# TensorE's order written out from chunk 4 on: whole tiles, one attention step between them, and the sums issued a chunk ahead

## The chip, the cores and the metric

The kernel runs on one core of one Trainium2 chip. Its engines are TensorE (PE, whose weight loads the profile lists as PEld), VectorE (DVE), ScalarE (ACT), GpSimd (POOL) and SyncE (SP, which issues most DMAs). Each of them takes its own instructions strictly in order; they wait for each other on semaphores. The metric is the device time of one execution in microseconds, the median over several runs.

## The reference

An attention of two parts feeds a gated feed-forward layer. q, k and v are 8 batches x 8 heads x 576 positions x 64.

```python
# coarse part: positions averaged in fours, full softmax attention over 144 of them, repeated back to 576
q_d = q.reshape(B, H, Sd, factor, D).mean(axis=3)          # k_d, v_d alike
out_up = np.repeat(sm_attn(q_d, k_d, v_d), factor, axis=2)
# local part: only |i - j| < 4, so seven neighbours of each position
scores = np.where(mask, scale * np.matmul(q, k.transpose(0, 1, 3, 2)), -1000000000.0)
out_local = np.matmul(softmax(scores), v)
x = (out_up + out_local).transpose(0, 2, 1, 3).reshape(B * S, H * D)     # 4608 tokens x 512
xn = x / np.sqrt(np.mean(x * x, axis=-1, keepdims=True) + 1e-06) * rms_g
g, val = xn @ w_gate, xn @ w_val                                          # 512 -> 1536
out = (g * (1 / (1 + np.exp(-g))) * val) @ w_out                          # 1536 -> 512
```

## The kernel before

The 4608 tokens are worked in 18 chunks of 256. A chunk's feed-forward layer (`Forward`) is cut into 12 tiles f of 128 hidden columns. Numbers are kept to more than one pass's accuracy by splitting a value into a high and a low part, so a tile has 24 first products on PE (`first`, L975: gate and value halves, four pieces of the inner dimension, three combinations of high and low each) and six second products (`second`, L1010: two halves of the tokens, three combinations). Between them stand ACT's tanh (L982), two DVE operations on the PSUM result (gate L985, product L990), ACT's high part (L996) and DVE's low part (L999). First products write one of three PSUM buffers ps_h; second products of all 12 tiles add up in two buffers ps_o, which ACT copies out (L1017) for a store (L1020). The parts hs have three buffers (LAG is 2).

While chunk c runs there, the local attention of chunk c+1 is made (`Attention`): eight scores on DVE (L757 and the sum L761), a softmax over the whole chunk (L771 to L795), eight values, each of which ACT (L804, eight small copies with a scale), DVE and POOL (L811) make in parts and DVE sums (L830); then the coarse part is added (L845), squares (L855) and a mean on PE (L862) give the norm (L866 to L896), and PE transposes x in eight pieces (`turn`, L906); ACT copies the result as the high part xh (L910), DVE takes the low part xl (L914). Only then can the chunk's first product start. The tiles x_t, up_t, q_t and prod have two buffers each, kv has four.

The coarse attention (`Coarse`) has 32 steps, one for each batch and pair of heads. One makes scores on PE (L499), a maximum (L508, L513 on DVE), exponentials (L518, ACT), turns on PE (L527), copies of them (L534, ACT), values on PE (L541), the scaling (L554, DVE) and a store to DRAM. Its q, k and v sums come by a first load on SP (L354, L358) and three accumulating DMAs each on POOL's queue (L362, `Sums`); two steps share one. Scores, turns, values, the mean and the transposes of x share three PSUM buffers ps_a. Chunks 4 to 11 carry two coarse steps each, chunk 3 one, chunks 12 to 17 none.

What sets the order: for the first three chunks a planner (`Plan`), whose choices stand as they are up to a given time. From the loop over chunks at the end of the function on (it starts at chunk index 3, the fourth), the program is only written in a likely order, with places in tiles (0.37, 3.0, 6.5, 10.4 and so on) for the attention's pieces, and the scheduler of the framework then decides the order on every engine, instruction by instruction. It may put six second products in two groups, or other work between the 24 first products of a tile.

Of the kernel before, what the change touches and what calls it, by code (L numbers as in the profile page):

```python
# [29 lines left out]
NF = DF // P  # L30
# [7 lines left out]
NCH = NU // 2  # L38
WPC = 512
LAG = 2  # L40
W_BUFS = 4
FIRST = 3
EARLY = 7
COARSE = {3: 1}
# [126 lines left out]
def attn_moe_kernel(  # L171
# [153 lines left out]
    up_dram, sums, stored = {}, {}, {}  # L325
# [109 lines left out]
    class Coarse:  # L435
# [3 lines left out]
            self.b, self.hp, self.pool, self.tag = b, hp, pool or ps_a, tag  # L439

        def steps(self):
            def low():
                if (self.b, self.hp // 2) not in sums:
                    sums[self.b, self.hp // 2] = Sums(self.b, self.hp // 2)
                self.sums = sums[self.b, self.hp // 2]
                self.scores()
                self.peak(0)
                self.peak(1)
                self.scale()
                self.powers(0)  # L450
                self.powers(1)

            def high():
                self.invert()
                for par in range(2):
                    self.turn(par)
                    self.copy(par)
                self.values()
                self.scaled()
                self.store()  # L460

            return low, high

        def plan(self, at, after=()):
            b, hp, tag = self.b, self.hp, self.tag
# [57 lines left out]
        def turn(self, par):  # L523
            tp = self.t[par] = self.pool.tile([HALF, 2, SD], FP32, name=self.tag)
            for kc in range(2):
                for c in range(2):
                    nc.tensor.transpose(  # L527
                        out=tp[:, kc, c * HALF:(c + 1) * HALF],
                        in_=self.a[par][:, c, kc * HALF:(kc + 1) * HALF],
                        identity=ident_sb[:HALF, :HALF],  # L530
                    )
# [39 lines left out]
    def window(t, s0, o0=0, o1=NO):  # L571
        b_ = t[:, :, :]
        return bass.AP(
            tensor=b_.tensor, offset=b_.offset + (s0 + o0) * D,
            ap=[b_.ap[0], [D, 2], [D, o1 - o0], [1, D]],
        )

    def bcast(ap, axis, n):
        shape = list(ap.shape)
        return ap.unsqueeze(axis).broadcast_to(shape[:axis] + [n] + shape[axis:])  # L580
# [4 lines left out]
    class Attention:  # L585
# [6 lines left out]
        def steps(self):  # L592
            def score(i):
                j, par, s0 = trio[i]
                if s0 == 0:
                    self.load_score(j, par)
                self.score(i)
                self.score_sum(i)

            def softmax():  # L600
                self.peak()
                self.less()
                self.powers()
                self.total()
                self.invert()
                self.shares()

            def value(i):
                j, par, s0 = trio[i]
                if s0 == 0:  # L610
                    self.load_value(j, par)
                self.value_scalar(i, 0)
                self.value_scalar(i, 1)
                self.value(i, "DVE", self.na, NO - self.np)
                self.value(i, "POOL", NO - self.np, NO)
                self.value_sum(i)

            def add(j):
                self.load_up(j)
                self.add_up(j)  # L620
                self.squares(j)

            def root():
                self.mean()
                self.rms()
                self.root("DVE")
                self.norm(0)
                self.norm(1)

            def turn(j):  # L630
                self.turn(j)
                self.high(j)
                self.low(j)

            todo = [(0.37 * i, lambda i=i: score(i)) for i in range(8)] + [(3.0, softmax)]
            todo += [(3.1 + 0.42 * i, lambda i=i: value(i)) for i in range(8)]
            todo += [(at, lambda j=j: add(j)) for j, at in enumerate((4.8, 6.4))]
            return todo + [(6.5, root), (10.4, lambda: turn(0)), (10.5, lambda: turn(1))]

        def plan(self, newton="POOL", before=()):  # L640
            c, np_, on_tensor, T = self.c, self.np, self.pt, due[self.c]
# [109 lines left out]
        def score(self, i):  # L751
            j, par, s0 = trio[i]
            if i == 0:
                self.sc = band.tile([P, 2, 2, US, NO], FP32, name="sc")
            q, k = self.qk[j, par]
            pr = self.pr[i] = band.tile([P, 2, NO, D], FP32, name="prod")
            nc.vector.tensor_tensor(out=pr, in0=bcast(q[:, s0:s0 + 2], 2, NO), in1=window(k, s0), op=ALU.mult)  # L757
# [50 lines left out]
        def value(self, i, engine, a, b):  # L808
            j, par, s0 = trio[i]
            p = self.sc[:, j, par, s0:s0 + 2]  # L810
            (nc.vector if engine == "DVE" else nc.gpsimd).tensor_tensor(  # L811
                out=self.pr[i][:, a:b], in0=bcast(p[:, :, a:b].rearrange("p s o -> p o s"), 3, D),
                in1=window(self.v[j, par], s0, a, b).rearrange("p s o d -> p o s d"), op=ALU.mult,
            )
# [211 lines left out]
    for fg in range(3):  # L1026
        for i in range(12):
            if i % 3 == 2 if fg < 2 else i >= 8:
                f = 4 * fg + (i // 3 if fg < 2 else i - 8)
                place[1, f] = len(pieces)  # L1030
                pieces.append(seconds[f])
            else:
                n = i - (i + 1) // 3 if fg < 2 else i
# [45 lines left out]
    coarse = [(b, hp) for b in range(B) for hp in range(KT)]  # L1079
# [4 lines left out]
    atts = [Attention(0, 1, 2, (ps_o, "ps_o")).plan("DVE")]  # L1084
    atts.append(Attention(1, 2, 2, (ps_a, "ps_a")).plan("DVE", [h.valued for h in opening] + atts[0].turns))
    done = 2 * KT
# [33 lines left out]

    att, late = atts[FIRST], []
    for c in range(FIRST, NCH):
        todo = []
        if c + 1 < NCH:
            nxt = Attention(c + 1)
            todo = nxt.steps()
            n = min(COARSE.get(c, 2), len(coarse) - done)
            for i, it in enumerate(coarse[done:done + n]):  # L1130
                at = 0.2 + 5.0 * i / n
                todo += zip((at + 0.1, at + 1.3), Coarse(*it).steps())
            done += n
            todo.sort(key=lambda t: t[0])
        fwd = Forward(att)
        for f in range(NF):
            fwd.emit(f)
            late.append((fwd, f))
            if len(late) > LAG:
                fw, g = late.pop(0)  # L1140
                fw.emit_second(g)
            while todo and todo[0][0] < f + 1:
                todo.pop(0)[1]()
        assert not todo
        att = nxt
    assert done == len(coarse)
    for fw, g in late:
        fw.emit_second(g)


# [52 lines left out]
```

## Time and profile before

| | |
|---|---|
| median of 3 runs | 1147.09 us (1144.93 to 1152.68) |
| profiled execution, first to last instruction | 1144.2 us; no other time of that execution is given |
| PE busy | 1082.0 us, 95% of the span, 8002 matmuls |
| DVE, ACT, POOL busy | 927.7, 624.1, 255.7 us |
| mean granted TensorE clock | 0.977 of full speed |
| matmuls of L975 / L1010 | 5184 / 1296 |
| DMA | 119.59 MB, 105 GB/s in the mean |

A matmul's busy time in the profile includes its pipeline, so rows of matmuls overlap: how fast they follow each other is read from their starts. The transposes of x begin 106 us into the span for the first chunk and 1082.6 us for the last. In the part of the timeline that is quoted below, the name of an operand tells the step: wg and wv belong to the first products, wo and hs to the second, qk to coarse scores, a_g with ident_sb to coarse turns, vs to coarse values, x_t with ident_sb to the transposes of x. A bracket at the end of a row gives the engine's idle time before it and what ended that.

### The profile page before, as it was taken

Reading aid. Unit: us, or ns where it says so; the run is one execution under the profiler, and the core shown is the slowest. Engines: PE = TensorE matmul, PEld = TensorE weight load, DVE = VectorE, ACT = ScalarE, POOL = GpSimd, SP = SyncE. Lnnn points to the kernel's source line nnn. Section 1 sums busy time; section 2 is a strip of 40 time slices with the busy share of each in tenths; the row PEclk is TensorE's granted clock in tenths of the full one; section 3 lists DMA queues with packets and bytes.
Section 4 is the critical chain, followed back from the end, with each engine's and each line's share of the span. In section 5 each row is a group of like instructions: output and inputs, shape, how many; then the busy total and the mean of one; then the engine's idle time right before and its main releaser. Section 6 shows DMA issues by size and latency. Waiting matters only on the chain.

```text
span 1144.2 us, 22238 instructions
## 1 busy us (share of the span) xinstructions
PE 1082.0 (95%) x8002; PEld 990.2 (87%) x8002; DVE 927.7 (81%) x1869; ACT 624.1 (55%) x2284; POOL 255.7 (22%) x317
## 2 busy tenths in 40 slices
PE   6883799999999899999999999999999999999998
PEld 4772698888899899999999999999999999999997
DVE  6787898778889989797979797979798989887432
ACT  1574673747392847474747474747475573837221
POOL 1554562334221211111111111101011020201000
PEclk9885999999999999999999999999999999999999
DMA  9985482446535353535263535222231313220000
GB/s 264 301 275 170 102 227 76 95 101 149 127 87 117 99 115 88 115 87 115 83 120 87 115 88 114 78 64 75 66 91 46 105 52 99 68 58 20 1 19 19
DMA packets 76815, 119.59 MB, mean 105 GB/s; under 512 B 26784, under 2 KB 36256, under 8 KB 76704
## 3 DMA queue, kind: packets, MB, share of 16 engines
q1 hardware_dynamic: 47520, 97.34, 28.8%
q0 software_dynamic: 8640, 15.93, 9.0%
q10 hardware_dynamic: 20544, 4.89, 2.0%
q8 instruction: 63, 1.03, 0.4%
q14 instruction: 48, 0.39, 0.1%
HBM read 106.33 MB, written 11.80 MB: 103 GB/s over the span
## 4 chain that ended last, share of the span: by engine, by line
PE 76%; DVE 9%; DMA 8%; ACT 3%; issue 3%; SPq 1%; POOL 1%; ACTq 0%; DVEq 0%; POOLq 0%
PE ps_h L975 46%; PE ps_o L1010 23%; PE ps_a L541 2%; DMA wg<-in_v_sum_dram 2%; DMA qk<-in_qk_sum_dram 2%; PE ps_a L499 2%; ACT prod L804 1%; DMA vs<-in_v_sum_dram 1%; PE ps_a L906 1%; DVE prod L757 1%; DVE o_sb L271 1%; PE ps_a L527 1%; DMA kv<-in_k_pad_dram 1%; DVE sc L761 1%; DMA up<-o_g 1%
## 5 line engine op out<-in xcount | busy, mean ns | idle before, releaser
L1010 PE MATMUL ps_o<-wo,hs 128*128 128x512 f32 x1296 | 356.0, 399 | 4.2 <-POOL hs L999 3.7
L975 PE MATMUL ps_h<-xh,wg 128*128 128x256 f32 x1728 | 348.2, 283 | 4.8 <-ACT xh L910 2.3
L975 PE MATMUL ps_h<-xh,wv 128*128 128x256 f32 x1728 | 343.0, 281 | 4.6 <-DVE sil L985 4.5
L975 PEld LDWEIGHTS ps_h<-xh,wg 128*128 128x128 f32 x1728 | 282.9, 190 | 14.2 <-ACT xh L910 3.0
L975 PEld LDWEIGHTS ps_h<-xh,wv 128*128 128x128 f32 x1728 | 281.9, 189 | 10.8 <-DVE sil L985 6.9
L804 ACT ACTIVATE prod<-kv,sc 128x64 f32<-128x64 f32 x1072 | 281.7, 408 | 13.0 <-DVE sc L795 4.8
L1010 PEld LDWEIGHTS ps_o<-wo,hs 128*128 128x128 f32 x1296 | 221.9, 188 | 41.4 <-POOL hs L999 6.2
L975 PE MATMUL ps_h<-xl,wg 128*128 128x256 f32 x864 | 244.8, 283 | 0.1
L975 PE MATMUL ps_h<-xl,wv 128*128 128x256 f32 x864 | 241.5, 280 | 0.0
L982 ACT ACTIVATE sil<-ps_h 128x256 f32<-128x256 f32 x216 | 82.9, 384 | 233.9 <-PE ps_h L975 208.8
L811 POOL TENSOR_TENSOR prod<-sc,kv 128x256 f32<-128x256 f32 x144 | 116.4, 843 | 397.4 <-DVE sc L795 175.4
L985 DVE SCALAR_TENSOR_TENSOR sil<-sil,ps_h 128x256 f32<-128x256 f32 x216 | 89.7, 415 | 103.1 <-ACT sil L982 91.0
L975 PEld LDWEIGHTS ps_h<-xl,wg 128*128 128x128 f32 x864 | 164.1, 190 | 6.9 <-issue 1.3
L975 PEld LDWEIGHTS ps_h<-xl,wv 128*128 128x128 f32 x864 | 163.6, 189 | 1.8
L996 ACT ACTIVATE hs<-sil 128x256 fp32r<-128x256 f32 x216 | 89.5, 416 | 136.9 <-DVE sil L990 122.4
L757 DVE TENSOR_TENSOR prod<-q_t,kv 128x896 f32<-128x896 f32 x140 | 151.7, 1086 | 5.6 <-DMA q_t<-in_q_band_dram 5.2
L830 DVE TENSOR_REDUCE x_t<-prod 128x128 f32<-128x896 f32 x128 | 136.8, 1077 | 23.6 <-ACT prod L804 16.4
L761 DVE TENSOR_REDUCE sc<-prod 128x14 f32<-128x896 f32 x144 | 154.5, 1077 | 0.4
L999 DVE TENSOR_TENSOR hs<-sil,hs 128x256 fp32r<-128x256 f32 x196 | 91.4, 466 | 29.5 <-ACT hs L996 29.2
L990 DVE SCALAR_TENSOR_TENSOR sil<-sil,ps_h 128x256 f32<-128x256 f32 x216 | 89.9, 416 | 8.1 <-PE ps_h L975 6.4
L362 POOL DMA_DIRECT2D qk<-in_qk_sum_dram x36 | 32.2, 895 | 187.3 <-DMA qk<-in_qk_sum_dram 111.8
L811 DVE TENSOR_TENSOR prod<-sc,kv 128x128 f32<-128x128 f32 (+2 forms) x144 | 69.5, 515 | 1.6 <-PE ps_o L826 0.8
(118 smaller groups left out, 984.3 us busy)
## 6 DMA issues: line engine op xcount, KB each, us to landing
kv<-in_k_pad_dram SPq DMA_DIRECT2D x72, 320.0 KB
kv<-in_v_pad_dram SPq DMA_DIRECT2D x72, 320.0 KB
qk<-in_qk_sum_dram POOLq DMA_DIRECT2D x36, 288.0 KB, 5.3
out_dram<-o_sb SPq DMA_DIRECT2D x36, 256.0 KB
q_t<-in_q_band_dram SPq DMA_DIRECT2D x70, 128.0 KB
vs<-in_v_sum_dram POOLq DMA_DIRECT2D x36, 144.0 KB, 3.5
qk<-in_qk_sum_dram SPq DMA_DIRECT2D x12, 288.0 KB
wo<-in_qk_sum_dram SPq DMA_DIRECT2D x2, 1152.0 KB
```

The lines of the kernel that those rows point to most:

```text
L757: nc.vector.tensor_tensor(out=pr, in0=bcast(q[:, s0:s0 + 2], 2, NO), in1=window(k, s0), op=ALU.mult)
L761: nc.vector.tensor_reduce(out=self.sc[:, j, par, s0:s0 + 2], in_=self.pr[i], axis=AX.X, op=ALU.add,)
L804: nc.scalar.activation(out=self.pr[i][:, o, s], in_=self.v[j, par][:, s0 + s + o], func=AF.Copy, scale=p[:, s, o:o + 1],)
L811: (nc.vector if engine == "DVE" else nc.gpsimd).tensor_tensor(out=self.pr[i][:, a:b], in0=bcast(p[:, :, a:b].rearrange("p s o -> p o s"), ...
L830: nc.vector.tensor_reduce(out=self.x[j][:, s0:s0 + 2, par], in_=pr.rearrange("p o s d -> p s d o"), axis=AX.X, op=ALU.add,)
L975: nc.tensor.matmul(out=self.p[f][:, t], lhsT=wi(f)[:, 0, k], rhs=xi[:, k], start=(n == 0), stop=(n == 3 * KT - 1),)
L982: nc.scalar.activation(out=self.sil[f], in_=self.p[f][:, 0], func=AF.Tanh, scale=0.5)
L985: nc.vector.scalar_tensor_tensor(out=self.sil[f], in0=self.sil[f], scalar=1.0, in1=self.p[f][:, 0], op0=ALU.add, op1=ALU.mult,)
L990: nc.vector.scalar_tensor_tensor(out=self.sil[f], in0=self.sil[f], scalar=0.5, in1=self.p[f][:, 1], op0=ALU.mult, op1=ALU.mult,)
L996: nc.scalar.activation(out=self.hs[f][:, 0], in_=self.sil[f], func=AF.Copy)
L999: (nc.gpsimd if engine == "POOL" else nc.vector).tensor_tensor(out=self.hs[f][:, 1], in0=self.sil[f], in1=self.hs[f][:, 0], op=ALU.subtract,)
L1010: nc.tensor.matmul(out=self.o[j], lhsT=lhs[:, cols], rhs=rhs(f)[:, 0], start=(f == 0 and i == 0), stop=(f == NF - 1 and i == 2),)
```

## The change

The loop over chunks now runs under a manual schedule for PE alone: PE's instructions stay in the order in which the program emits them, and the scheduler places only those of the other engines. The loop is therefore written out for PE. Each tile emits its 24 first products, then the attention step due in that slot, then six second products. Tile f's second products follow the first products of tile f+2; those of tile 10 follow tile 11's, and those of tile 11 stand behind the first tile of the next chunk. A coarse step has three slots now, scores, turns and values, two tiles apart: the first step in tiles 0, 2 and 4, the second in 4, 6 and 8. The mean and the norm come in tile 8. The eight transposes of x come as one step in tile 11, behind its first products and ahead of 12 second products; before, they stood behind tile 10. The sums of the next two coarse steps are issued one chunk ahead (`sums_for`). No computation is added or taken away.

```diff
@@ Coarse.steps
-            def low():
-                if (self.b, self.hp // 2) not in sums:
-                    sums[self.b, self.hp // 2] = Sums(self.b, self.hp // 2)
+            def score():
                 self.sums = sums[self.b, self.hp // 2]
                 self.scores()
...
-            def high():
-                self.invert()
+            def turn():
                 for par in range(2):
                     self.turn(par)
                     self.copy(par)
+                self.invert()
+
+            def value():
                 self.values()
                 self.scaled()
                 self.store()
 
-            return low, high
+            return score, turn, value
@@ Attention.steps
-            def turn(j):
-                self.turn(j)
-                self.high(j)
-                self.low(j)
+            def turn():
+                self.turn(0)
+                self.turn(1)
+                for j in range(2):
+                    self.high(j)
+                    self.low(j)
...
-            return todo + [(6.5, root), (10.4, lambda: turn(0)), (10.5, lambda: turn(1))]
+            return todo, root, turn
@@ the loop over chunks
-    att, late = atts[FIRST], []
-    for c in range(FIRST, NCH):
...
-            n = min(COARSE.get(c, 2), len(coarse) - done)
-            for i, it in enumerate(coarse[done:done + n]):
-                at = 0.2 + 5.0 * i / n
-                todo += zip((at + 0.1, at + 1.3), Coarse(*it).steps())
...
-            late.append((fwd, f))
-            if len(late) > LAG:
-                fw, g = late.pop(0)
-                fw.emit_second(g)
...
+    def sums_for(n):
+        for b, hp in coarse[n:n + 2]:
+            if (b, hp // 2) not in sums:
+                sums[b, hp // 2] = Sums(b, hp // 2)
+
+    att, before = atts[FIRST], None
+    with tc.manual_schedule(engines={mybir.EngineType.PE}):
+        for c in range(FIRST, NCH):
+            fwd = Forward(att)
+            todo, slots = [], {f: [] for f in range(NF)}
+            if c + 1 < NCH:
+                nxt = Attention(c + 1)
+                todo, root, turn = nxt.steps()
+                n = min(COARSE.get(c, 2), len(coarse) - done)
+                for at, it in zip((0, 4), coarse[done:done + n]):
+                    for f, step in zip((at, at + 2, at + 4), Coarse(*it).steps()):
+                        slots[f].append(step)
+                done += n
+                sums_for(done)
+                slots[8].append(root)
+                slots[NF - 1].append(turn)
+                todo.sort(key=lambda t: t[0])
+            for f in range(NF):
+                fwd.emit(f)
+                for step in slots[f]:
+                    step()
+                if f == 0 and before:
+                    before.emit_second(NF - 1)
+                if f >= LAG:
+                    fwd.emit_second(f - LAG)
+                if f == NF - 1:
+                    fwd.emit_second(NF - 2)
+                while todo and todo[0][0] < f + 1:
+                    todo.pop(0)[1]()
```

Lines behind L600 carry numbers two higher in the changed kernel: L975 is L977, L1010 is L1012, L906 is L908, and so on.

The first place is PE at the start of a chunk with coarse steps, around the first coarse scores (L499). Before, word for word:

```order
L975 MATMUL ps_h<-xh,wg_0_408 128x256
L1010 MATMUL ps_o<-wo_2_1576,hs 128x512
L1010 MATMUL ps_o<-wo_2_1577,hs 128x512
L1010 MATMUL ps_o<-wo_2_1576,hs 128x512
L1010 MATMUL ps_o<-wo_2_1577,hs 128x512
L499 MATMUL ps_a<-qk 72x144 x2
L1010 MATMUL ps_o<-wo_2_1576,hs 128x512 x2
L975 MATMUL ps_h<-xh,wg_0_408 128x256
L499 MATMUL ps_a<-qk 72x144 x2
L975 MATMUL ps_h<-xl,wg_0_408 128x256
```

The scores stand in two pairs, and both the second products of the old chunk's tile 11 and tile 0's first products are cut for them. The same place on PE in the changed kernel:

```order
L977 MATMUL ps_h<-xh,wv_0_416 128x256
L499 MATMUL ps_a<-qk 72x144 x4
L1012 MATMUL ps_o<-wo_2_1576,hs 128x512
L1012 MATMUL ps_o<-wo_2_1577,hs 128x512
L1012 MATMUL ps_o<-wo_2_1576,hs 128x512 x2
L1012 MATMUL ps_o<-wo_2_1577,hs 128x512
L1012 MATMUL ps_o<-wo_2_1576,hs 128x512
L977 MATMUL ps_h<-xh,wg_0_408 128x256
```

All of tile 0's first products now stand ahead of the four scores, and the six second products behind them are whole. 

The second place is DVE around the low part of x (L914, later L916), where a chunk turns into the next. Before:

```order
L990 SCALAR_TENSOR_TENSOR sil<-sil,ps_h 128x256
L830 TENSOR_REDUCE x_t<-prod 128x2x64 x2
L999 TENSOR_TENSOR hs<-sil,hs 128x256
L914 TENSOR_TENSOR xl<-ps_a,xh 128x4x128 x2
L811 TENSOR_TENSOR prod<-sc,kv 128x128 x2
L830 TENSOR_REDUCE x_t<-prod 128x2x64
```

Here L830 are value sums of the chunk after the one that is transposed, and L990 and L999 belong to tile 10. In the changed kernel the same place on DVE reads:

```order
L832 TENSOR_REDUCE x_t<-prod 128x2x64
L987 SCALAR_TENSOR_TENSOR sil<-sil,ps_h 128x256
L832 TENSOR_REDUCE x_t<-prod 128x2x64
L916 TENSOR_TENSOR xl<-ps_a,xh 128x4x128 x2
L813 TENSOR_TENSOR prod<-sc,kv 128x128
L992 SCALAR_TENSOR_TENSOR sil<-sil,ps_h 128x256
L813 TENSOR_TENSOR prod<-sc,kv 128x128
L832 TENSOR_REDUCE x_t<-prod 128x2x64 x2
```

The gate of tile 11 (L987) now stands between the two value sums, and its product (L992) behind xl.

The third place is ACT behind the high part of x (L910, later L912), up to the exponentials (L518) of the chunk's first coarse step. Before:

```order
L910 CAST xh<-ps_a 128x4x128 x2
L804 ACTIVATE prod<-kv,sc 128x64 x16
L982 ACTIVATE sil<-ps_h 128x256
L804 ACTIVATE prod<-kv,sc 128x64 x16
L855 ACTIVATE up_t,ss<-x_t 128x128
L996 ACTIVATE hs<-sil 128x256
L982 ACTIVATE sil<-ps_h 128x256
L855 ACTIVATE up_t,ss<-x_t 128x128
L804 ACTIVATE prod<-kv,sc 128x64 x2
L518 ACTIVATE a_g,z_g<-ps_a,m_g 72x144 x4
```

34 value copies and two squares stand between xh and the exponentials. In the changed kernel ACT has, in the same place:

```order
L912 CAST xh<-ps_a 128x4x128 x2
L806 ACTIVATE prod<-kv,sc 128x64 x16
L998 ACTIVATE hs<-sil 128x256
L806 ACTIVATE prod<-kv,sc 128x64 x9
L984 ACTIVATE sil<-ps_h 128x256
L806 ACTIVATE prod<-kv,sc 128x64 x7
L857 ACTIVATE up_t,ss<-x_t 128x128
L1019 COPY o_sb<-ps_o 128x512 x2
L806 ACTIVATE prod<-kv,sc 128x64 x7
L857 ACTIVATE up_t,ss<-x_t 128x128
L518 ACTIVATE a_g,z_g<-ps_a,m_g 72x144 x3
L998 ACTIVATE hs<-sil 128x256
```

Now 39 value copies and the two output copies (L1019) stand ahead of them, and tile 0's high part (L998) ahead of the last exponential.

More of the change, by code (lines that the diff above doesn't have):

```diff
@@ L1119, in attn_moe_kernel @@
     plan.run()
-    att, late = atts[FIRST], []
-    for c in range(FIRST, NCH):
[L1125 to L1128, printed above, removed]
-            n = min(COARSE.get(c, 2), len(coarse) - done)
-            for i, it in enumerate(coarse[done:done + n]):
-                at = 0.2 + 5.0 * i / n
-                todo += zip((at + 0.1, at + 1.3), Coarse(*it).steps())
[L1133 to L1137, printed above, removed]
-            late.append((fwd, f))
-            if len(late) > LAG:
-                fw, g = late.pop(0)
-                fw.emit_second(g)
[L1142 to L1145, printed above, removed]
@@ L1146, in attn_moe_kernel @@
-    assert done == len(coarse)
-    for fw, g in late:
-        fw.emit_second(g)
+    def sums_for(n):
[31 more added lines that the diff above has]
+                    todo.pop(0)[1]()
+            assert not todo
+            att, before = nxt, fwd
+        assert done == len(coarse)
+        before.emit_second(NF - 1)
```

## The prediction

> **What bounds the kernel now.** I read the stretches of one chunk first, since shares over the whole span mix the opening with the steady part. A chunk is the time from one group of turn transposes (L906) to the next. The first row below is a chunk that also carries two coarse steps (chunks 4 to 11), the second one without (12 to 16); columns: length, PE, PEld, DVE, ACT, POOL busy, granted clock, DMA share, GB/s.
>
> ```profile
> 714.85:772.03 57.18, 57.18 (x436) 52.63 (x436) 47.94 (x105) 33.39 (x130) 6.09 (x8) 1.00 0.26 71
> 931.04:981.95 50.91, 50.91 (x373) 47.82 (x372) 45.78 (x93) 28.90 (x110) 6.55 (x8) 1.00 0.27 76
> ```
>
> PE has a matmul in flight for all of 57.18 and 50.91 us, at full clock; DVE is busy for 84% and 90%. So PE bounds, and only a shorter PE stream or a new PE wait can move these 13 chunks. What a tile costs when nothing interrupts it stands at the end of the chain of waits (start, us, engine, line):
>
> ```profile
> 1104.23 2.75 PE ps_h L975 x24
> 1108.35 2.75 PE ps_h L975 x24
> ```
>
> From one to the next it is 4.12 us: 24 first products and six second products. Twelve are 49.44 us; the rest of a chunk is turns, coarse steps and what cutting costs. The timeline of PE has these (start, length of the group, line, operands, count):
>
> ```profile
> 712.43 1.54 PE L1010 MATMUL ps_o<-wo,hs 128*128 128x512 f32 x6
> 713.81 1.04 PE L906 MATMUL ps_a<-ident_sb,x_t 128*128 128x128 f32 x8
> 714.60 0.37 PE L975 MATMUL ps_h<-xh,wg 128*128 128x256 f32 x1
> ...
> 719.92 0.71 PE L499 MATMUL ps_a<-qk 64*72 64x144 f32 x4
> 720.55 0.73 PE L1010 MATMUL ps_o<-wo,hs 128*128 128x512 f32 x2
> ...
> 721.33 0.71 PE L499 MATMUL ps_a<-qk 64*72 64x144 f32 x4
> 721.97 0.39 PE L975 MATMUL ps_h<-xl,wg 128*128 128x256 f32 x1
> ...
> 730.17 0.41 PE L527 MATMUL ps_a<-ident_sb,a_g 72*72 72x72 f32 x4
> 730.39 0.36 PE L975 MATMUL ps_h<-xl,wg 128*128 128x256 f32 x1
> 730.59 0.35 PE L527 MATMUL ps_a<-ident_sb,a_g 72*72 72x72 f32 x3
> 730.75 0.36 PE L975 MATMUL ps_h<-xh,wg 128*128 128x256 f32 x1
> 730.95 0.28 PE L975 MATMUL ps_h<-xh,wv 128*128 128x256 f32 x1
> ...
> 732.36 0.28 PE L975 MATMUL ps_h<-xh,wg 128*128 128x256 f32 x1
> ...
> 737.05 1.20 PE L541 MATMUL ps_a<-vs,a_g 72*72 72x64 f32 x16
> ...
> 738.47 0.71 PE L499 MATMUL ps_a<-qk 64*72 64x144 f32 x8
> 739.11 1.65 PE L1010 MATMUL ps_o<-wo,hs 128*128 128x512 f32 x6
> ```
>
> **What whole steps save.** Coarse scores (L499) cut in two take 719.92 to 720.55 and 721.33 to 721.97, 1.27 us; the uncut ones in the same chunk 738.47 to 739.11, 0.64. Turns (L527) in pieces cost little themselves, but the first product behind each piece takes 0.20 (730.39 to 730.59) where the mean is 0.115. The uncut sum of a coarse chunk: 49.44; the turn transposes 0.79 (713.81 to 714.60) and 0.08 behind them; the mean 0.2 (estimate from the turns' rows); two scores at 0.64 and 0.2 for the changes before and behind, 1.7; two sets of turns, eight at 0.055 (730.17 to 730.39 is four) and 0.1, 1.1; two sets of values (L541) at 1.0 and 0.1, 2.2. That is 55.5 against 57.2: **-1.7 us x 8 = -13.6**. A chunk without coarse steps: 49.44 + 0.87 + 0.2 = 50.5 against 50.91: **-0.4 x 5 = -2.0**.
>
> **What the fixed order costs.** An engine takes its instructions in order, so PE now waits where it used to have other work. The rows of DVE and ACT around the same turn:
>
> ```profile
> 714.51 2.08 DVE L830 TENSOR_REDUCE x_t<-prod 128x128 f32<-128x896 f32 x2 [0.53 <-PE ps_a L906]
> 716.51 0.42 DVE L999 TENSOR_TENSOR hs<-sil,hs 128x256 fp32r<-128x256 f32 x1
> 716.84 1.28 DVE L914 TENSOR_TENSOR xl<-ps_a,xh 128x512 fp32r<-128x512 f32 x2
> ...
> 720.91 0.41 DVE L985 SCALAR_TENSOR_TENSOR sil<-sil,ps_h 128x256 f32<-128x256 f32 x1
> 721.24 0.44 DVE L508 TENSOR_REDUCE m_g<-ps_a 72x2 f32<-72x288 f32 x1
> ...
> 730.80 1.08 DVE L757 TENSOR_TENSOR prod<-q_t,kv 128x896 f32<-128x896 f32 x1
> 731.80 0.42 DVE L999 TENSOR_TENSOR hs<-sil,hs 128x256 fp32r<-128x256 f32 x1
> ```
>
> *The turn.* The first value sum (L830) waits for the first four transposes (its bracket): they free the x_t that it writes. Nothing behind it on DVE can pass it. From the start of the transposes: value sum at 0.70, 1.0 (two start 2.0 before the next row); a gate 0.33 (720.91 to 721.24); the second value sum 1.0; two xl copies 1.28. xl is whole at 4.31. In the trace it was whole at 718.12 and first read at 721.97. Now PE has behind the transposes (0.79) 12 second products, 2 x 1.37 (712.43 to 713.81), and one first product that reads xh alone, 0.12: it wants xl at 3.65 and waits **0.66, at 13 turns +8.6**. From below 0.66 would be 0 if the value sum came after xl, but the order of DVE puts it ahead.
>
> ```profile
> 714.45 1.07 ACT L910 CAST xh<-ps_a 128x512 fp32r<-128x512 f32 x2
> ...
> 719.54 0.37 ACT L982 ACTIVATE sil<-ps_h 128x256 f32<-128x256 f32 x1
> 719.81 3.99 ACT L804 ACTIVATE prod<-kv,sc 128x64 f32<-128x64 f32 x16
> 723.63 0.29 ACT L855 ACTIVATE up_t<-x_t 128x128 f32<-128x128 f32 x1
> ...
> 723.92 0.40 ACT L996 ACTIVATE hs<-sil 128x256 fp32r<-128x256 f32 x1
> ...
> 726.03 0.37 ACT L518 ACTIVATE a_g<-ps_a,m_g 72x144 f32<-72x144 f32 x1
> ...
> 726.39 0.37 ACT L518 ACTIVATE a_g<-ps_a,m_g 72x144 f32<-72x144 f32 x1
> ...
> 731.96 1.12 ACT L1017 COPY o_sb<-ps_o 128x512 f32<-128x512 f32 x2
> ```
>
> *The first coarse step and tiles 0 and 1.* Behind xh, which is done 1.65 after the transposes begin, ACT's new order has ahead of the last exponential 39 value copies (L804, 16 in 3.82: 9.3), two high halves and a tanh at 0.3, two squares at 0.29, two output copies 1.0, four exponentials at 0.36: 13.2 us, and about 0.3 for a product buffer that a value sum still holds. It ends at 15.3. PE would get to its second set of turns at 0.79 + 2.74 + 0.66 + 2.87 (tile 0) + 0.86 (scores) + 1.37 + 5.56 (tiles 1, 2) + 0.3 = 15.15: a wait of 0.2. From there DVE has before tile 1's low half (L999): inverses 0.3, gate 0.33, value sum 1.0, product 0.35, score 1.0 (730.80 to 731.80), gate, score sum 1.0, value sum 1.0, product, and the half itself 0.4, 6.1 in all; PE has turns 0.3, second products 1.45, tile 3 at 2.78, two second products 0.46, 5.0. It waits 1.1. So **1.3 x 8 = +10.4**. Bounds: 0, if ACT's copies start before xh; 3, if each of the three sums there runs a further 0.5 late.
>
> *Chunks without coarse steps.* No scores lie between tile 0 and tile 11's second products: they want the low half at 0.79 + 2.74 + 0.66 + 2.8 + 0.46 = 7.45, and DVE reaches it at 4.31 + 0.8 (two value pieces, a product) + 2.0 (value sums) + 0.6 = 7.7. By the same count tile 0 waits 0.3 and tile 1 0.3: **0.9 x 5 = +4.5**.
>
> *Chunks 3 and 4*, where DVE still lags:
>
> ```profile
> 377.08 0.62 PE L975 MATMUL ps_h<-xh,wg 128*128 128x256 f32 x3 [1.62 <-ACT xh L910]
> ...
> 375.00:380.00 5.00, 2.82 (x16) 2.20 (x15) 4.55 (x8) 5.00 (x18) 1.86 (x2) 0.89 0.55 170
> 380.00:385.00 5.00, 5.00 (x36) 5.00 (x35) 4.93 (x10) 5.00 (x24) 2.51 (x3) 0.76 0.26 70
> ```
>
> There PE used to empty its second products before the turn; now 18 of them (4.1 us) stay behind it and fill the 1.62. Between -3 (wait and slow clock gone) and +4.1: I take **+1**.
>
> *The sums.* Their loads (SP) and three accumulations each (POOL) come up to a chunk earlier. On POOL two of them now stand between the second and third value piece, and each waits for the one before to land:
>
> ```profile
> 709.09 0.83 POOL L362 DMA_DIRECT2D vs<-in_v_sum_dram  x1 [2.69 <-DMA vs<-in_v_sum_dram]
> ```
> ```profile
> vs<-in_v_sum_dram POOLq DMA_DIRECT2D x36, 144.0 KB, 3.5
> ```
>
> Two such steps, 3.5 us to landing in the median (the page's DMA issues, last number), start some 10 us before the turn, while the third piece can only begin once the turn has freed a value sum: 0, and if they are late by 1 us, +8. SP's load of the last k goes behind the output stores; its scores come over 20 us later: 0.
>
> Sum: -15.6 + 8.6 + 10.4 + 4.5 + 1 = +8.9 on the profiled 1144.2, so 1153.1. The median of the runs is 2.9 above that span; with it 1156.
>
> **The rivals.** *No new wait* (0.24): ACT and DVE keep the lead they have; in both stretches above PE has no wait at all. Then -15.6, 1131.5. Against it stands the value sum's bracket. *First products stay slow* (0.19): twelve of them take 1.41 after the cut turns (730.95 to 732.36), 0.1175 each, against 0.1145 in the uncut tiles; coarse chunks have this over long stretches, and I counted it as a cost of cuts. If it is one of ACT's and DVE's load instead, up to 288 x 0.0035 = 1.0 a chunk isn't saved, 8 more; with it 1164, slower. It decides from 3 us on. *The clock* (0.12): the row of 380 to 385 shows 0.76 granted after waits of which the longest is 1.62, that stretch and the one before losing 5 x 0.24 + 5 x 0.11 = 1.75 us. Waits of 0.66, 0.2 and 1.1 in 20 us are less dense; if they trip it at each of 13 turns, +22.8, 1179. [...] *The change does less than it says*: excluded by the rows of the order, where PE's scores, turns and second products stand whole from chunk 4 on.
>
> **How the numbers follow.** The forecast has 0.42, 0.03 is for the unforeseen. About 1% (11.5 us) can be told from no change; the forecast, +0.8%, lies just under it, and its own range is 1147 to 1165 (the bounds of the first coarse step and of the early chunks). Faster by 1%: the first rival and a tail, 0.25. Slower: the slow products, the clock and a quarter of the forecast less a little, 0.38. Same: 0.37. The range reaches from the first rival to beyond the slow products: 1130 to 1172; the clock and half a tenth elsewhere stay out.
>
> **What would show it.** Right: PE waits of 0.5 to 1 us for xl (L916 now) once a chunk, and about 1 us for hs or a_g in the first 25 us of a chunk; coarse chunks near 57.5 us, the others near 52; L499 always in eights at 0.64. Wrong: a chunk under 56 us, PE without waits (first rival), or a granted clock under 1.00 after chunk 5.

## The result and the profile after

The changed kernel takes 1176.96 us, the median of four runs (1175.46 to 1177.74); the kernel before, run beside it, 1147.93. The ratio is 1.0249, with a 95% interval of 1.0222 to 1.0276: slower. The prediction was 1156, in a range of 1130 to 1172. It had the sign of the most likely case right, and the size far too small.

The profiled execution has a span of 1173.7 us, 29.5 more than before, and its own time is 1175.46. DVE's low half of a tile is L1001 here. To find where the 29.5 us lie I cut both spans at the same transposes of x: chunks 3 and 4, chunks 5 to 11, chunks 12 to 16, and the rest. First before, then after; the columns are those of the chunk rows in the prediction.

```profile
312.81:427.79 114.98, 111.66 (x834) 102.60 (x835) 103.09 (x218) 69.61 (x273) 24.50 (x30) 0.99 0.44 104
427.79:828.18 400.39, 400.39 (x3040) 368.20 (x3038) 338.40 (x733) 233.84 (x903) 67.74 (x86) 1.00 0.38 92
828.18:1082.60 254.42, 254.42 (x1852) 239.04 (x1850) 212.90 (x439) 139.69 (x528) 29.94 (x38) 1.00 0.22 61
1082.60:1144.20 61.60, 57.34 (x411) 53.32 (x409) 18.36 (x43) 14.05 (x33) 0.00 (x0) 0.99 0.05 18
```
```profile
312.33:433.69 121.36, 115.19 (x860) 105.60 (x858) 104.32 (x219) 70.40 (x274) 24.13 (x30) 0.97 0.42 98
433.69:839.40 405.71, 394.90 (x3040) 363.95 (x3039) 351.59 (x732) 234.38 (x903) 66.72 (x86) 1.00 0.38 92
839.40:1115.28 275.88, 263.15 (x1852) 240.54 (x1851) 217.21 (x437) 142.95 (x528) 28.55 (x38) 0.99 0.19 56
1115.28:1173.69 58.41, 54.58 (x388) 50.54 (x386) 17.56 (x41) 13.62 (x32) 0.00 (x0) 1.00 0.05 19
```

Chunks 3 and 4 grew by 6.4, but they hold 26 more PE instructions and the rest 23 fewer (first numbers in brackets): the turn now stands behind tile 11 and not behind tile 10, so a tile has moved from the end to here. With the -3.2 of the rest this is +3.2. The seven chunks 5 to 11, all with coarse steps, grew by 5.3, 0.76 each. **The five chunks without coarse steps grew by 21.5**, 4.3 each. Up to the cut at 312 there is a difference of -0.5.

PE had no gap in these two stretches before (its busy time was their length); now it has. Its waits in chunks 5 to 11, and then in 12 to 16 (total us, times, longest):

```profile
PE ps_o L1012 <- DVE hs L1001: 7.4, 7, 1.1
PE ps_h L977 <- DVE xl L916: 3.2, 7, 0.5
```
```profile
PE ps_o L1012 <- DVE hs L1001: 10.3, 9, 2.2
PE ps_h L977 <- DVE xl L916: 2.2, 5, 0.5
```

In a coarse chunk they are the two waits that the prediction named, one for xl behind the turn, one for tile 1's low half. The timeline of PE, chunk 10:

```profile
727.15 0.28 PE L977 MATMUL ps_h<-xh,wg 128*128 128x256 f32 x1
727.89 0.38 PE L977 MATMUL ps_h<-xl,wg 128*128 128x256 f32 x1 [0.46 <-DVE xl L916]
...
743.25 0.62 PE L1012 MATMUL ps_o<-wo,hs 128*128 128x512 f32 x2
744.94 1.20 PE L1012 MATMUL ps_o<-wo,hs 128*128 128x512 f32 x4 [1.06 <-DVE hs L1001]
```

A bracket gives idle time, counted from the end of the row before (727.43 for the first). What a wait costs is read from the starts and is a little more: from 727.15 to 727.89 it is 0.74, where a first product follows the one before in 0.115, so the wait for xl costs 0.62. The two second products at 743.25 take 0.46 and the next starts 1.69 behind them, so tile 1's half costs 1.23.

In a chunk without coarse steps there is another, twice as long, at tile 2. PE and then DVE in chunk 14, whose transposes begin at 951.27:

```profile
965.48 0.62 PE L1012 MATMUL ps_o<-wo,hs 128*128 128x512 f32 x2
966.45 1.19 PE L1012 MATMUL ps_o<-wo,hs 128*128 128x512 f32 x4 [0.34 <-DVE hs L1001]
...
974.77 0.73 PE L1012 MATMUL ps_o<-wo,hs 128*128 128x512 f32 x2
977.68 1.20 PE L1012 MATMUL ps_o<-wo,hs 128*128 128x512 f32 x4 [2.18 <-DVE hs L1001]
```
```profile
970.29 0.42 DVE L1001 TENSOR_TENSOR hs<-sil,hs 128x256 fp32r<-128x256 f32 x1
970.62 0.68 DVE L847 TENSOR_TENSOR x_t<-x_t,up_t 128x512 f32<-128x512 f32 x1
971.23 2.08 DVE L759 TENSOR_TENSOR prod<-q_t,kv 128x896 f32<-128x896 f32 x2
...
973.89 2.07 DVE L763 TENSOR_REDUCE sc<-prod 128x14 f32<-128x896 f32 x2
975.88 0.41 DVE L992 SCALAR_TENSOR_TENSOR sil<-sil,ps_h 128x256 f32<-128x256 f32 x1
976.21 1.08 DVE L759 TENSOR_TENSOR prod<-q_t,kv 128x896 f32<-128x896 f32 x1
977.21 0.41 DVE L1001 TENSOR_TENSOR hs<-sil,hs 128x256 fp32r<-128x256 f32 x1
```

Between tile 1's low half (970.29) and tile 2's (977.21) lie 6.92 us, since DVE does the addition and five score operations of a microsecond each (L759, L763) in between. PE needs the half after one tile and stands 2.18 us. From start to start the wait for xl, the short one at tile 0 (966.45) and this one cost 0.6, 0.5 and 2.4 us, 3.5 of the 4.2 by which chunk 14 grew. Before, DVE had the same habit, and the low halves (then L999) were as far apart:

```profile
941.25 0.42 DVE L999 TENSOR_TENSOR hs<-sil,hs 128x256 fp32r<-128x256 f32 x1
...
947.74 0.42 DVE L999 TENSOR_TENSOR hs<-sil,hs 128x256 fp32r<-128x256 f32 x1
```

PE in the same place of the kernel before:

```profile
944.48 0.63 PE L1010 MATMUL ps_o<-wo,hs 128*128 128x512 f32 x2
...
948.70 1.08 PE L1010 MATMUL ps_o<-wo,hs 128*128 128x512 f32 x4
```

6.49 us between two tiles of 4.12, and PE had no wait: the scheduler had cut the six second products, and first products fill the 4 us between the two that need the high half alone and the four that stand behind the low half. That freedom is what the change took away.

The last chunk of the group points at the cause before any experiment. Chunk 16 has no scores to make on DVE (none of L759 in it, against eight in chunk 15), and it grew by 1.3 us only, from 50.78 to 52.10:

```profile
1006.42:1063.18 56.76, 8.56 (x8) 0.97 0.20 58
1063.18:1115.28 52.10, 0.00 (x0) 1.00 0.03 11
```

(Length, DVE's busy time in L759, clock, DMA share, GB/s.) Chunk 15 also shows a clock of 0.97. The granted clock was 0.50 for 3.41 us in it and in chunk 12, which costs by estimate 1.7 us (half of 3.41) twice; the section on the hardware comes back to this.

So there are two things to test: that PE's waits in a fixed order are the loss, and that the place of the low halves in DVE's order, not DVE's load, makes them.

### The profile page after: what moved, and what is told of

Same layout as the page of the kernel before. It is cut to its first block, busy times and chain, and to the rows that moved or that the text cites. A ratio compares the mean times of both kernels' runs of the same rounds, so it can differ in the third digit from the quotient of the medians.

```text
span 1173.7 us, 22241 instructions
## 1 busy us (share of the span) xinstructions
PE 1086.6 (93%) x8002; PEld 988.2 (84%) x8002; DVE 945.2 (81%) x1869; ACT 627.9 (54%) x2284; POOL 253.3 (22%) x317
## 4 chain that ended last, share of the span: by engine, by line
PE 55%; DVE 16%; ACT 14%; DMA 7%; issue 6%; POOL 1%; SPq 1%; ACTq 0%; DVEq 0%; POOLq 0%
PE ps_h L977 33%; PE ps_o L1012 16%; ACT prod L806 10%; DVE x_t L832 3%; DVE prod L759 3%; DMA qk<-in_qk_sum_dram 2%; PE ps_a L541 2%; DMA wg<-in_v_sum_dram 2%; DVE hs L1001 1%; DVE o_sb L271 1%; ACT a_g L518 1%; DVE sil L987 1%; ACT o_sb L1019 1%; DVE sc L763 1%; DVE sil L992 1%
## 5 line engine op out<-in xcount | busy, mean ns | idle before, releaser
L1012 PE MATMUL ps_o<-wo,hs 128*128 128x512 f32 x1296 | 347.3, 402 | 25.3 <-DVE hs L1001 20.5
L977 PE MATMUL ps_h<-xh,wg 128*128 128x256 f32 x1728 | 342.8, 283 | 3.1 <-DVE wg L295 1.8
L977 PE MATMUL ps_h<-xh,wv 128*128 128x256 f32 x1728 | 334.5, 279 | 2.7 <-DVE sil L987 2.6
L977 PEld LDWEIGHTS ps_h<-xh,wg 128*128 128x128 f32 x1728 | 283.6, 192 | 11.8 <-DVE wg L295 2.0
L1012 PEld LDWEIGHTS ps_o<-wo,hs 128*128 128x128 f32 x1296 | 225.8, 188 | 80.3 <-DVE hs L1001 32.1
L977 PEld LDWEIGHTS ps_h<-xh,wv 128*128 128x128 f32 x1728 | 278.6, 189 | 6.1 <-DVE sil L987 4.9
L977 PE MATMUL ps_h<-xl,wg 128*128 128x256 f32 x864 | 245.6, 284 | 6.0 <-DVE xl L916 6.0
L977 PE MATMUL ps_h<-xl,wv 128*128 128x256 f32 x864 | 240.2, 278 | 0.0
L813 POOL TENSOR_TENSOR prod<-sc,kv 128x256 f32<-128x256 f32 x144 | 112.9, 811 | 433.5 <-DVE sc L797 134.2
L977 PEld LDWEIGHTS ps_h<-xl,wg 128*128 128x128 f32 x864 | 166.0, 192 | 17.4 <-DVE xl L916 10.5
L998 ACT ACTIVATE hs<-sil 128x256 fp32r<-128x256 f32 x216 | 89.8, 416 | 154.2 <-DVE sil L992 147.7
L832 DVE TENSOR_REDUCE x_t<-prod 128x128 f32<-128x896 f32 x128 | 136.5, 1075 | 42.7 <-PE ps_a L908 29.5
L977 PEld LDWEIGHTS ps_h<-xl,wv 128*128 128x128 f32 x864 | 163.5, 189 | 0.3
L987 DVE SCALAR_TENSOR_TENSOR sil<-sil,ps_h 128x256 f32<-128x256 f32 x216 | 89.1, 413 | 90.9 <-ACT sil L984 78.5
L759 DVE TENSOR_TENSOR prod<-q_t,kv 128x896 f32<-128x896 f32 x140 | 151.9, 1087 | 5.8 <-DMA q_t<-in_q_band_dram 5.5
L763 DVE TENSOR_REDUCE sc<-prod 128x14 f32<-128x896 f32 x144 | 154.3, 1076 | 0.4
L1001 DVE TENSOR_TENSOR hs<-sil,hs 128x256 fp32r<-128x256 f32 x196 | 93.7, 479 | 34.5 <-ACT hs L998 34.4
L992 DVE SCALAR_TENSOR_TENSOR sil<-sil,ps_h 128x256 f32<-128x256 f32 x216 | 89.2, 413 | 6.4 <-PE ps_h L977 4.5
L813 DVE TENSOR_TENSOR prod<-sc,kv 128x128 f32<-128x128 f32 (+2 forms) x144 | 75.1, 542 | 0.7 <-PE ps_o L828 0.2
```

The source lines that it names most:

```text
L763: nc.vector.tensor_reduce(out=self.sc[:, j, par, s0:s0 + 2], in_=self.pr[i], axis=AX.X, op=ALU.add,)
L832: nc.vector.tensor_reduce(out=self.x[j][:, s0:s0 + 2, par], in_=pr.rearrange("p o s d -> p s d o"), axis=AX.X, op=ALU.add,)
L977: nc.tensor.matmul(out=self.p[f][:, t], lhsT=wi(f)[:, 0, k], rhs=xi[:, k], start=(n == 0), stop=(n == 3 * KT - 1),)
L987: nc.vector.scalar_tensor_tensor(out=self.sil[f], in0=self.sil[f], scalar=1.0, in1=self.p[f][:, 0], op0=ALU.add, op1=ALU.mult,)
L992: nc.vector.scalar_tensor_tensor(out=self.sil[f], in0=self.sil[f], scalar=0.5, in1=self.p[f][:, 1], op0=ALU.mult, op1=ALU.mult,)
L998: nc.scalar.activation(out=self.hs[f][:, 0], in_=self.sil[f], func=AF.Copy)
```

## The experiments

Theory A: the fixed order makes PE stand before second products whose low half DVE brings late (and, by 0.45 us a chunk, before xl). Theory B: the sums issued a chunk ahead, or what the earlier chunks do, are behind it. Theory C: DVE's load or slower first products are, and the waits only show it. Each was run against the kernel before on the same chip.

**The sums alone.** The kernel before, with the sums moved a chunk ahead:

```diff
+    def sums_for(n):
+        for b, hp in coarse[n:n + 2]:
+            if (b, hp // 2) not in sums:
+                sums[b, hp // 2] = Sums(b, hp // 2)
...
             done += n
+            sums_for(done)
```

> The kernel before, with the sums issued a chunk ahead as the only edit; the scheduler orders TensorE everywhere. Theory A (fixed order): no difference from the kernel before, 1148, give or take 4. Theory B (the sums' accumulations on GpSimd's queue hold up the value pieces): slower by up to 8 us, 1156, in the chunks with coarse steps.

1147.17 us, a ratio of 0.9998 (0.9975 to 1.0021). The sums cost nothing there. Nor do they in the fixed order of the changed kernel: chunk 8, with six accumulations on GpSimd's queue, takes 57.91 us, and chunk 10, with none, 57.96. That half of B is out.

**The loop as it is written, with PE's order free.**

```diff
-    with tc.manual_schedule(engines={mybir.EngineType.PE}):
+    if True:
```

> The changed kernel's loop as it is written (steps in three parts, sums a chunk ahead, the same order of emission), but with TensorE's order left to the scheduler as well. Theory A (only the fixing of TensorE's order costs time): 1148 to 1153, without waits of TensorE for hs or xl in the steady chunks; the slow end of this allows for the 52.2 us that chunks 12 to 15 took when the scheduler had them in this loop. Rival (the way the loop is written moves VectorE's and ScalarE's work, and that is what makes the halves late): 1165 to 1177.

(The 52.2 us in it come from the next run, which was made first.)

1153.33 us, 1.0053 (1.0035 to 1.0072). So 0.5%, some 6 us, comes from the loop as it is written, and fixing PE's order in this loop adds the other 23 or 24 of the 29. A coarse chunk is 56.88 here (57.18 before) and another 52.14 (50.91), with waits of 0.3 us for xl and for the squares. The five chunks without coarse steps are 5.4 us longer in all (259.87, 254.42 before), about as much as the whole difference; the expectation allowed for them in its slow end, 1153, which is where it came out.

```profile
937.68:989.82 52.14, 51.50 (x372) 47.93 (x371) 45.15 (x92) 29.01 (x109) 5.79 (x8) 1.00 0.26 74
```

**Fixed for chunks 4 to 11 only.** (The loop's chunk 3 is fixed as well.)

```diff
-    with tc.manual_schedule(engines={mybir.EngineType.PE}):
-        for c in range(FIRST, NCH):
+    for c in range(FIRST, NCH):
+        with (tc.manual_schedule(engines={mybir.EngineType.PE}) if c < 12 else ExitStack()):
```

> TensorE's order is fixed for chunks 4 to 11 alone; chunks 12 to 16 go back to the scheduler's order, all else is as in the changed kernel. Theory A (TensorE, in its fixed order, stands before the second products of tile 2, whose low half comes late on VectorE; most of this is in the chunks without coarse steps): these five chunks fall from 55.2 to 56.8 us back to about 51, which is 21.5 us less, the end of the kernel gives back some 3, and the time is about 1158. Theory B (the sums issued a chunk ahead, or the whole steps of the earlier chunks, leave the last chunks behind): the last five chunks stay at 55 or more, and the time at 1175 or so.

1164.35 us, 1.0142 (1.0097 to 1.0186). The five last chunks fell from 275.9 to 260.1 us (840.21 to 1100.28) while nothing ahead of them changed: a coarse chunk is still 57.90, with the same two waits. What the earlier chunks do is therefore not behind the greater part, 15.8 of 21.5 us, and theory B's second half is out for that. They did not come back to 254.4: four of them are 52.2, as in the free order above, and this is why 1164 and not 1158.

```profile
666.47:724.37 57.90, 56.32 (x436) 51.92 (x435) 50.12 (x104) 33.56 (x129) 11.12 (x14) 1.00 0.44 101
944.55:996.77 52.22, 51.59 (x373) 48.00 (x372) 45.16 (x92) 29.01 (x109) 5.73 (x8) 1.00 0.27 74
```

**Second products one tile later.** The three buffers of hs stay; the high and low parts of a tile are emitted behind the second products that free their buffer.

```diff
-                if f == 0 and before:
-                    before.emit_second(NF - 1)
-                if f >= LAG:
-                    fwd.emit_second(f - LAG)
+                if f < 2 and before:
+                    before.emit_second(NF - 2 + f)
+                if f >= LAG + 1:
+                    fwd.emit_second(f - LAG - 1)
+                fwd.emit_parts(f)
                 if f == NF - 1:
-                    fwd.emit_second(NF - 2)
+                    fwd.emit_second(NF - 3)
```

> The changed kernel with every tile's second products one tile later in TensorE's order (tile 10's behind the next chunk's tile 0, tile 11's behind tile 1); what VectorE and ScalarE do is the same. Theory A: the waits before second products go (1.06 us in each of eight chunks with coarse steps; about 2.8 us in each of five without, and the half clock that came with them, 1.7 us twice), while the wait for xl stays at 0.45: 1177 - 8.5 - 14 - 3.4 = 1151, between 1143 and 1157. Theory C (the loss lies in the whole steps or in slower first products, and the waits before second products only show a delay that VectorE has anyway): the waits move to another instruction and the time stays above 1170.

1146.33 us, 0.9982 (0.9958 to 1.0007): 31 us less than the changed kernel, level with the kernel before. A coarse chunk is 56.59, another 51.36. PE's only wait from 440 to 1093 us is that for xl:

```profile
PE ps_h L979 <- DVE xl L916: 5.5, 12, 0.5
```

(The lines behind the new function stand two further down once more: L979 is the first product, L1003 the low half.) The waits before second products have gone and moved nowhere, as A says; a load on DVE that was too large would have shown them a tile later. The halves themselves are no more regular than before. Two of them in a chunk without coarse steps, one behind the other, are still 6.25 us apart:

```profile
958.44 0.42 DVE L1003 TENSOR_TENSOR hs<-sil,hs 128x256 fp32r<-128x256 f32 x1
...
964.69 0.42 DVE L1003 TENSOR_TENSOR hs<-sil,hs 128x256 fp32r<-128x256 f32 x1
```

Now PE does not stand for them. One thing is not as the expectation has it: with the parts emitted at another place, DVE's order is not quite that of the changed kernel, so the run does not move the lag alone.

**The turn a tile earlier.**

```diff
-                slots[NF - 1].append(turn)
+                slots[NF - 2].append(turn)
```

> The changed kernel with the turn (transposes, high and low parts of x) behind tile 10's first products and not behind tile 11's, so that there is a tile more of TensorE's work (4.1 us) between it and the next chunk's first products. Theory A: the wait for xl (0.45 us at 13 turns) goes, and VectorE and ScalarE start the next chunk's work a tile earlier, so that the low halves of tiles 1 and 2 are there in time: 1177 - 6 - 8.5 - 12 - 3.4 = 1147. If the normalised rows come too late for an earlier turn, TensorE waits before the transposes and part is given back: up to 1165. Theory C (VectorE itself is the bound of these chunks): the time stays above 1170.

1190.86 us, 1.0379 (1.0335 to 1.0423). I had expected 1147, so this was wrong by its sign. The wait for xl did go, but PE now waits for low halves 30 times, 33.3 us from 434 to 1125. The row of the waits, and DVE behind the transposes of a coarse chunk (494.87):

```profile
PE ps_o L1012 <- DVE hs L1001: 33.3, 30, 2.8
```
```profile
496.90 1.08 DVE L832 TENSOR_REDUCE x_t<-prod 128x128 f32<-128x896 f32 x1
497.90 1.28 DVE L916 TENSOR_TENSOR xl<-ps_a,xh 128x512 fp32r<-128x512 f32 x2
...
500.49 2.05 DVE L832 TENSOR_REDUCE x_t<-prod 128x128 f32<-128x896 f32 x2
...
502.67 0.41 DVE L1001 TENSOR_TENSOR hs<-sil,hs 128x256 fp32r<-128x256 f32 x1
```

The earlier turn starts the next chunk's value sums earlier, and DVE does them ahead of the low half of tile 10 (502.67), which PE wants behind tile 11's first products: it stands 1.27 us for it. I had counted xl's cover and forgotten what the turn releases. The number alone fits theory C ("above 1170"), but the same turn with one tile of lag, below, runs without any wait, so it is the place again and not the load.

**The low halves on GpSimd.**

```diff
-            self.low(f, "DVE")
+            self.low(f, "POOL")
```

> The changed kernel, its order on TensorE untouched, with the low halves of the steady chunks taken on GpSimd (0.87 us each where the opening has them there) and not on VectorE. Theory A (what is late is not the work but the place of the low half in VectorE's order, behind score operations): the 2.2 us wait at tile 2 goes in the five chunks without coarse steps, with the two spells of half clock: 1177 - 13 - 3 = 1161, and to 1153 if the 1.06 us of the coarse chunks goes as well. Against it in coarse chunks: the low half can now stand behind a sum's accumulation on GpSimd's queue, which waits for the one before to land (3.5 us), and the gain there is lost again, 1165 to 1175. Theory C (VectorE as a whole is late): tile 2 still waits, because its product comes late as well; above 1170.

1197.3 us, 1.0437 (1.0411 to 1.0464): slower than both cases that I gave for theory A; by the number alone it would be C's "above 1170". The chunks say why it is not. Below stand one coarse chunk in which sums are accumulated on GpSimd's queue (six times), one in which none are, and one without coarse steps.

```profile
639.71:702.57 62.86, 58.10 (x437) 53.35 (x436) 47.45 (x92) 33.84 (x129) 20.53 (x26) 0.97 0.40 92
766.67:823.34 56.67, 56.22 (x437) 52.06 (x435) 47.45 (x92) 33.53 (x129) 15.39 (x20) 1.00 0.27 72
984.55:1036.57 52.02, 51.50 (x372) 47.30 (x371) 43.63 (x80) 29.10 (x109) 16.12 (x20) 1.00 0.26 74
```
Where no accumulation is on GpSimd's queue, it goes as theory A has it: with PE's order untouched, the 2.2 us wait has gone and the chunks without coarse steps fall from 55.15 to between 52.02 and 52.33, and the coarse one from 57.96 to 56.67 (PE's only wait from 766 us on is for xl, 0.5 us each). Since this edit also takes work off DVE, it does not by itself tell the place from the load; the runs with one tile of lag do. Where six accumulations are, GpSimd waits for transfers to land (for qk 13 times, 5.0 us at the longest, in the rows below), the low halves stand behind, PE waits up to 4.7 us, and the granted clock is below 1.00 too (0.97 in the mean of that row, 0.95 in that of the next chunk). I had priced that at what the change gains; it is 5 to 6 us more than in the changed kernel in each of six chunks.

```profile
PE ps_o L1012 <- POOL hs L1001: 22.1, 5, 4.7
...
POOL qk L362 <- DMA qk<-in_qk_sum_dram: 54.6, 13, 5.0
```

**One tile later, with 18 second products behind the turn.** Tile 10's second products stay with those of tiles 8 and 9; against the run with one tile of lag:

```diff
-                if f < 2 and before:
-                    before.emit_second(NF - 2 + f)
+                if f == 1 and before:
+                    before.emit_second(NF - 1)
...
                     fwd.emit_second(NF - 3)
+                    fwd.emit_second(NF - 2)
```

> As the one-tile-later experiment, but tile 10's second products stay behind the turn with those of tiles 8 and 9, so that 18 of them (4.1 us) and not 12 stand between the transposes and the next chunk's first products; tile 11's stay behind the next chunk's tile 1. Theory A (TensorE's waits on VectorE are what the fixed order costs): the wait for xl, 0.45 us at 13 turns, goes too, and nothing new comes: 1146 - 6 = 1140, faster than the kernel before by 0.7%, with coarse chunks at 56.1 and the others at 50.9. Theory C (first products run slower whatever stands in front of them): the 0.45 us reappears as longer tiles, 1146.

1139.23 us, 0.9922 (0.9901 to 0.9944), **faster than both kernels**, than the one before by 0.8%, with the chunks as expected and no gap on PE from 438 to 1083 us:

```profile
660.81:716.75 55.94, 55.94 (x436) 52.31 (x435) 49.14 (x104) 32.94 (x129) 12.41 (x14) 1.00 0.46 104
930.71:981.69 50.98, 50.98 (x372) 47.59 (x371) 46.08 (x92) 29.23 (x109) 6.81 (x8) 1.00 0.27 76
```

**One tile later, and the turn a tile earlier.** Both edits above.

> Second products one tile later and the turn behind tile 10. In the run with the turn alone moved, VectorE's xl and value sums came ahead of the low halves of tiles 10, 0, 1 and 2 and TensorE waited up to 2.8 us for them; one tile of lag is 4.1 us. Theory A: all these waits and the one for xl vanish: 1146 - 6 = 1140, and up to 4 us less if the first products stay as fast as in the run with the turn alone moved (115.5 ns each against 117). Rival: VectorE falls behind by more than a tile, waits of about 1 us remain before tile 1's or 2's second products, 1155.

1140.82 us, 0.9941 (0.9921 to 0.9960). No gap either from 432 to 1076 us; the coarse chunks are the shortest of all runs:

```profile
656.39:712.17 55.78, 55.78 (x437) 52.16 (x436) 49.00 (x104) 33.12 (x129) 11.59 (x15) 1.00 0.44 104
924.79:975.32 50.53, 50.53 (x372) 47.55 (x371) 46.52 (x92) 28.83 (x109) 5.79 (x8) 1.00 0.27 76
```

The rival's waits did not come. The two kernels' intervals overlap, so which of them is faster is open. In these rows DVE does the same work as in the changed kernel and is busier (49.00 of 55.78 us and 46.52 of 50.53, against 50.06 of 57.96 and 46.17 of 55.15), while PE waits for nothing: DVE's load is out as the cause of the loss. Slower first products, the rest of theory C, are out as well. From start to start, two of the twelve tiles of chunk 10 in the changed kernel take 0.1177 us a product and the others, the wait for xl apart, 0.114; before, seven of the twelve of the same chunk took 0.117 to 0.118 where one first product follows another.

## Why the prediction was wrong

- **What whole steps save: right, a little large.** 1.7 us in a coarse chunk and 0.4 in another were worked out from an uncut sum of 55.5 and 50.5 us. The last run, in which PE waits for nothing, has 55.78 and 50.53: 1.4 and 0.4. Without waits the fixed order is worth 13 us in 13 chunks, where 15.6 were counted.
- **The turn: right.** 0.66 us was predicted, counted from start to start; measured so it is 0.62, with PE idle for 0.46 of it. The value sum stands ahead of xl as described.
- **The first coarse step: right.** 1.1 us at tile 1's low half was predicted, 1.23 measured from start to start (1.06 idle). The 0.2 before the second turns is 0.25: in chunk 10 the first step's eight turns take 0.71 (738.32 to 739.03), the second step's 0.46. The sum for a coarse chunk was +0.26 (-1.7 + 0.66 + 1.3); +0.76 came, 0.3 of the difference from the smaller saving.
- **Chunks without coarse steps: the step that failed.** The prediction put the wait for tile 2's low half at nothing, without a reason. It had +4.5 for the waits before second products, 0.9 a chunk, from tiles 11, 0 and 1; with the other terms +1.16 a chunk. It came to +4.3, a miss of 15.7 in five chunks, of a miss of 20.6 in the profiled span (1173.7 against 1153.1). The walk along DVE ended at tile 1. It should have gone on as long as DVE still had the next attention's work in front of a low half: tile 2's stands behind five score operations, and this wait alone is 2.18 us of idle time and costs 2.4. In chunk 16, which has no scores, the prediction's sum (+1.16) holds, with +1.3 measured. Each microsecond needed for it was on hand: the score operations had a row, and the low halves of before, 6.49 us apart, showed the place.
- **The clock: not counted, and it came twice.** The rival had it at each of 13 turns, for waits of 0.66 us; in chunks 5 to 11, with such a wait in each (0.46 us of idle time in the mean), it stayed at 1.00. It was 0.50 for 3.41 us behind each of two waits of 2.18 us, in chunks 12 and 15, by estimate 3.4 us of time in all, inside the 21.5. Waits, counted from start to start, and clock together are some 18 of the 21.5. Second products also follow each other more slowly, 0.243 us apart in the mean of chunk 14 where the kernel before has 0.231; why is open.
- *First products stay slow*, the rival that would have kept coarse chunks long, did not come, as said above.
- **Chunks 3 and 4**: +1 predicted, +3.2 with the tile that moved there from the end. **The sums**: 0 predicted, 0 measured.
- **The range** took in no case for these chunks beyond what the walk gave: no bound above was put on their waits, though the coarse step had one. The rival without new waits (1131.5) is what the last two experiments come near to, by one more tile of lag; they reached 1139 and 1141 because the whole steps saved less and chunks 3 and 4 cost more than it had.

What stays open: why the loop as it is written costs 6 us with PE's order left free, most of it in chunks 12 to 16, for which I have only the 0.3 us waits; and whether DVE's order alone, changed with everything else kept, would give the same as the lag. A version that moves only the score operations on DVE was not tried; the low halves on GpSimd come nearest to it.

## What to carry over

When an engine's order is fixed by hand, give every operand of its instructions a due time, and walk the supplying engine's queue through a whole period and not only to the first wait. What decided here was the latest delivery against its due time (6.92 us between two low halves, tiles of 4.12), not the mean load. One more tile of lag cost no buffer and turned 2.5% slower into level with the kernel before; with the wait for xl covered too it was 0.8% faster. Without that lag, an earlier turn or the move to an idler queue (GpSimd, busy for 22% of the changed kernel's span where DVE is for 81%) made the whole slower, since each put other work in front of the same operand, the second in the chunks with accumulations.

## What the runs showed of the hardware

In chunks 12 and 15 of the changed kernel the granted clock was 0.50 for 3.41 us each time. The two stretches begin at 866.68 and 1033.93, 49 such lengths apart. The rows below cut the span into stretches of this length, counted from there (length, PE, PEld, DVE, ACT, POOL busy, granted clock, DMA share, GB/s):

```profile
863.27:866.68 3.41, 1.23 (x6) 0.73 (x5) 3.41 (x6) 0.42 (x1) 0.00 (x0) 1.00 0.26 74
866.68:870.09 3.41, 3.41 (x17) 3.32 (x16) 3.41 (x6) 0.42 (x1) 0.00 (x0) 0.50 0.43 123
...
975.91:979.32 3.41, 1.64 (x10) 1.46 (x11) 3.41 (x8) 0.42 (x1) 0.00 (x0) 1.00 0.22 54
979.32:982.74 3.42, 3.42 (x27) 3.22 (x26) 3.42 (x5) 0.80 (x2) 0.00 (x0) 1.00 0.28 91
```

The first pair is chunk 12, where the 2.18 us wait falls into one stretch: PE is busy for 1.23 us of it (1.24 in chunk 15), and the clock in the next is 0.50. The second is chunk 14: the same wait, split by the border of two stretches, leaves 1.64 us busy, and the clock stays at 1.00. In the run with PE's order free, chunk 4 has a stretch with 1.93 us busy, and half the clock in the next two:

```profile
376.11:379.53 3.42, 1.93 (x13) 1.28 (x12) 3.01 (x7) 3.42 (x14) 0.54 (x1) 1.00 0.00 0
379.53:382.94 3.41, 2.30 (x8) 1.67 (x9) 3.02 (x6) 3.41 (x14) 1.33 (x2) 0.50 0.80 246
382.94:386.35 3.41, 3.41 (x16) 3.41 (x17) 3.38 (x7) 3.41 (x16) 1.70 (x2) 0.50 0.18 31
```

So 0.50 came behind 1.93 us busy there, and 1.00 behind 1.64 here: busy time alone does not tell these cases apart, and what else counts, the runs do not show. PE was not idle throughout: in the stretch ahead of the half clock it has matmuls in flight for 36% of the time in chunk 12 (1.23 us), and for 56% in chunk 4 of the other run. Of the four waits of 2.2 us in this kernel, the two that lie in one stretch (chunks 12 and 15) had 3.41 us at 0.50 behind them, by estimate 1.7 us on top of their own length; the two that a border splits (chunk 13, at 921.29, and chunk 14) had none. Four cases do not show that the border decides it.
